# Summing the attention block's e @ x for two or three sets of rows at once in a fused attention and SwiGLU kernel on Trainium2

## The chip, the core and the metric

The kernel runs on one core of one Trainium2 chip. The core has a matrix engine (TensorE, "PE" in the profile, with its weight loads shown apart as "PEld"), a vector engine (VectorE, "DVE"), a scalar engine (ScalarE, "ACT"), a general engine (GpSimd, "POOL"), and a queue engine (SyncE, "SP") that here only issues transfers. [...]The metric is the device time of the whole kernel in microseconds, the median of several runs.

## What is computed

Two blocks follow each other. The first is an attention through 32 inducing rows, for each of 4 batches of 12416 rows of 128 numbers; the second is a gated feed-forward network over all 49664 rows.

```
def mab(q, kv):
    s = scale * (q @ kv.transpose(0, 2, 1))
    a = exp(s - s.max(-1));  a /= a.sum(-1) + 1e-9
    return a @ kv
h   = mab(inducing, x)          # per batch: 32 x 128
y   = mab(x, h)                 # per batch: 12416 x 128
xn  = y / rms(y) * rms_g
out = (silu(xn @ w_gate) * (xn @ w_val)) @ w_out     # 128 -> 1536 -> 128
```

The change is in `h`: with `e = exp(s - max)`, the unnormalised `e @ x` of a batch sums over its 12416 rows. Everything is in float32, partly by splitting numbers in parts.

## The kernel before

**Sets, units and slots.** The 97 tiles of 128 rows of a batch are cut into seven sets: five of 16 tiles, one of 15, one of 2 (`per`, lines 81 to 85). The feed-forward network walks a batch in 25 units of up to 512 rows (four to a set, one for the last rows), and each unit in 12 slots `j`, one for each 128 columns of the 1536. So a batch has 300 slots, numbered `k` from 0; four batches have 1200.

**A slot** (`slot`, lines 654 to 678) is, on TensorE: the gate product `g` (line 656), then one earlier slot's product with `w_out`, then the value product `v` (line 667), then whatever other steps the plan has put in this slot. ScalarE takes silu of `g` (line 664), VectorE multiplies it with `v` into a tile `u` (line 673). The product with `w_out` is taken some five slots later, in one of two ways. A plain one is a float32 matmul (line 605, `acc<-u,wo`; the trace shows it as two passes). A split one is three matmuls (lines 621, 623 and 605, `acc<-xn,xn`) over parts of `u` that ScalarE and GpSimd prepare (lines 643 to 649). I call these plain and split slots. When a unit's twelve products are in, VectorE adds and turns the result (lines 613 and 614) and SP stores it (line 636). SP also fetches the moving operand `a` of the next unit (line 551, four transfers, at `j` = 2 of each unit).

**The attention of the next batch runs inside the slots of the present one.** `schedule` (lines 781 to 844) is an order written out by hand: `add(k, step, ...)` puts a step behind slot `k`. For the next batch it loads `x` transposed (line 152) and makes scores; at slots 130 to 136 it takes the maximum and the exponentials; between slots 140 and 190 it forms `h`; from slot 200 on the second scores. So this happens in batches 0, 1 and 2, for batches 1, 2 and 3. The first batch's own attention stands ahead of the first slot and is not changed in what it issues.

**Forming h.** Three steps for each set `s`:
- `load_rows(b, s)` (line 135): four transfers of 32 partitions each, on SP (line 141). 256 KB each for a full set. The sets share two buffers by turns, `xn0` and `xn1`; the last set, of two tiles, has its own, `xn6`. So the load of set 2 waits until TensorE has read set 0.
- `turn_e(s)` (line 369): VectorE transposes the set's exponentials into a tile `e` of the pool `work`, which has three buffers, shared with the tiles `eT`, `z` and `aT` of the step that prepares the next units (`seam`, lines 489 to 541).
- `sum_h(s)` (line 374): for each tile of the set a matmul of 32 columns of `e` with 128 x 128 of `x` (line 384), into one of four 32-partition strips of one bank of the accumulator memory, taken by turns, so that four strips gather four partial sums. Each matmul shows as two passes. Then VectorE copies the bank to `hl` for set 0 and adds it to `hl` for the others (lines 387, 389).

Before the change the steps stand at slots 140 + 7s (turn), 143 + 7s (sum), and 97, 103, then 130 + 7s (load): seven sums at 143, 150, 157, 164, 171, 178 and 185. `fold_l`, `divide` and `turn_h`, which use the result, stand at 187, 189 and 191. The bank comes from a pool with a single buffer (`ps_m`), shared with other steps, among them `square` of the seam at slot 161.

**Which slots are split** is worked out ahead by a small budget of GpSimd's time (lines 870 to 882); the sums have no part in it, so it is the same before and after.

Of the kernel before, what the change touches and what calls it, by code (L numbers as in the profile page):

```python
# [9 lines left out]
F32 = mybir.dt.float32  # L10
# [4 lines left out]
ALU = mybir.AluOpType  # L15
# [3 lines left out]
P = 128  # L19
R = 4  # L20
# [4 lines left out]
def kernel(  # L25
# [45 lines left out]
    nc = tc.nc  # L71
    B, N, C = x.shape
    m = inducing.shape[0]
# [7 lines left out]
    full, rest = divmod(N // P, 16)  # L81
    assert N % P == 0 and full >= 2 and 0 < rest < 4
    per = [16] * (full - 1) + [15, rest + 1]
    NS = len(per)
    start = [P * sum(per[:s]) for s in range(NS)]
# [18 lines left out]
    def pool(name, bufs, **kw):  # L104
        return ctx.enter_context(tc.tile_pool(name=name, bufs=bufs, **kw))
# [8 lines left out]
    work = pool("work", 3)  # L114
    once = pool("once", 1)
# [17 lines left out]
    xnat, xT = {}, {}  # L133
# [57 lines left out]
    ps = ps_m.tile([P, 512], F32, name="mm", tag="mm")  # L191
# [10 lines left out]
    if wide:  # L202
        t = scp.tile([P, SCW], F32, name="sc")
# [89 lines left out]
    def attention(b, load_next):  # L293

        st = {}
# [7 lines left out]
        def bank():  # L303
            if flowing:
                assert not lent
                return ps_m.tile([P, 512], F32, name="mm", tag="mm")
            return ps_gv.tile([P, 512], F32, name="gv", tag="gv")
# [59 lines left out]
                nc.vector.reduce_sum(out=st["hl"][:, C:C + 1], in_=st["ls"][:, 0:k + 1], axis=AX.X)  # L367

        def turn_e(s):
            e = st["e", s] = (work.tile([P, per[s] * m], F32, name="e", tag="work") if b else  # L370
                              up.tile([P, 512], F32, name="u"))[:, 0:per[s] * m]
            nc.vector.transpose(out=e, in_=sc[b][:, cols1[s]])

        def sum_h(s):

            n = per[s]
            e, xn, hl = st.pop(("e", s)), xnat.pop((b, s)), st["hl"]
            if b or not s:
                st["ps"] = bank()
            ps = st["ps"]  # L380
            head, end = (True, True) if b else (s == 0, s + 1 == NS)
            for t in range(n):
                more = t + R < n or not b and any(per[z] > t % R for z in range(s + 1, NS))
                nc.tensor.matmul(ps[ts(t % R, m), 0:C], e[:, ts(t, m)], xn[:, t, :], start=head and t < R, stop=not more)  # L384
            rows = slice(0, min(n, R) * m)
            if end and head and s:
                nc.vector.tensor_tensor(out=hl[rows, 0:C], in0=hl[rows, 0:C], in1=ps[rows, 0:C], op=ALU.add)
            elif end and b:
                nc.vector.tensor_copy(out=hl[:, 0:C], in_=ps[:, 0:C])

        def fold_l():
# [323 lines left out]
    one = weight[1, 0]  # L715
# [27 lines left out]
    ps = f["scores"](0, f["st"]["hT"][:, 0:m], R, per2[0])  # L743
# [37 lines left out]
    def schedule(b):  # L781


        plan, marks, busy = {}, [], {}

        def add(k, step, *args):
            plan.setdefault(int(k), []).append(lambda: step(*args))
            if getattr(step, "__name__", "") == "sub_max" and args[0]:
                busy[int(k)] = 1.1

        def exponentials(k, step, first):

            groups = list(range(first, NS - 1, 2))
            for i, s in enumerate(groups):
                add(k + i, step, s, NS if s == groups[-1] else s + 2)
                if i:
                    by_tanh.add((b, k + i))
            return k

        if not b:  # L800
            add(0, weight[1, 1]["sign"])
            add(1, weight[1, 1]["lower"])
            for k, one in ((1, (2, 1)), (5, (0, 2)), (8, (1, 2)), (11, (2, 2))):
                for j, name in ((0, "power"), (1, "power_number"), (1, "upper"), (2, "upper_number"), (2, "sign"), (3, "lower")):
                    add(k + j, weight[one][name])
            for k, *one in ((2, 0, 1), (4, 1, 1), (11, 0, 2), (13, 1, 2)):
                add(k, f["stack_of"], *one)
                add(k, f["stack_low"], *one)
            for step in range(4):
                add(18 + 2 * step, split_wo, step)  # L810
            for s in range(1, NS):
                add(2 * s + 16, f["scores2"], s)
                add(2 * s + 17, f["row_max"], s)
                add(2 * s + 18, f["sub_max"], s)
            marks.append(exponentials(3 * NS + 9, f["exp2"], 1))
        if b + 1 < B:
            g = attention(b + 1, b + 2 < B)
            for k, one in enumerate(pieces[b + 1]):
                add(6 * k if b else 13 + 3.8 * k, load_channels, *one)
            add(0, g["open_"])  # L820
            for s in range(NS):
                at = 20 + 14 * s if b else 37 + 12 * s
                for k in range(R):
                    add(at + 3 * k, g["turn_x"], s, k)
                add(at + 14, g["scores1"], s)
                add(97 + 6 * s if s < 2 else 130 + 7 * s, load_rows, b + 1, s)
                add(140 + 7 * s, g["turn_e"], s)
                add(143 + 7 * s, g["sum_h"], s)
                add(200 + 7 * s, g["scores2"], s)
                add(203 + 7 * s, g["row_max"], s)  # L830
                add(204 + 7 * s, g["sub_max"], s)
            for k, name in ((126, "max1"), (128, "max2"), (130, "max3"), (187, "fold_l"), (189, "divide"), (191, "turn_h"),
                            (193, "square_h")):
                add(k, g[name])
            for i in range(2):
                add(175 + 23 * i, g["fetch"], i)
                add(197 + 7 * i, g["stack"], i)
                for k in range(R):
                    add(199 + 7 * i + k, g["place"], i, k)
            marks += [exponentials(134, g["exp1_of"], 0), exponentials(254, g["exp2"], 0)]  # L840
        if b + 2 < B:
            for k in range(215, NU * NJ, 6):
                add(k, load_channels, *pieces[b + 2].pop(0))
        return plan, marks, busy
# [3 lines left out]
    order = [(b, s) for b in range(B) for s in range(NS)]  # L848
    firsts = {s: min(u for u, one in enumerate(units) if one[0] == s) for s in range(NS)}
    for k, (b, s) in enumerate(order):  # L850
# [5 lines left out]
        for late_by, one in enumerate(following):  # L856
            for i, step in enumerate(seam(*one)):
                j = ((14, 17, 18, 21, 21, 29, 31) if k else (32, 33, 34, 35, 35, 39, 41))[i]
                n, j = divmod(j, NJ)
# [4 lines left out]
    flat = [(b, u) for b in range(B) for u in range(NU)]  # L864
    after = dict(zip(flat, flat[1:]))
    plans = [schedule(b) for b in range(B)]

    free, ready = 0.0, {}  # L870
    for b, u in flat:
        plan, marks, busy = plans[b]
        for j in range(NJ):
# [3 lines left out]
            begin = max(free, now + 2.2 * SLOT)  # L877
# [6 lines left out]
    for b in range(B):  # L884
        plan, marks, _ = plans[b]

        order = [(u, j) for u in range(NU) for j in range(NJ)]
# [72 lines left out]
```

## Time and profile before

| | |
|---|---|
| median of 4 runs | 1667.05 us (1665.98 to 1667.82) |
| the profiled execution | 1667.82 us, its span 1666.0 us |
| TensorE busy | 1652.7 us, 99% of the span |
| ScalarE, VectorE, GpSimd busy | 1236.6, 1174.8, 1158.6 us |
| granted TensorE clock | 1.000 |
| matmuls of the sums in the slots, line 384 | 582 passes |
| first slots of batches 0, 1, 2, 3 | about 57, 474, 879 and 1284 us |

How to read it: a row of a group gives line, engine, operation, output and input, shape and count, then busy time and mean duration, then the idle time of the engine ahead of these instructions and what ended it. In the timeline a row is start, length, engine, line, operation; several like instructions in a row are merged into one, with a count. Matmuls are pipelined: the length of one says little, the distance from one start to the next says what it costs. The start of a batch's slots is needed to find a slot: in batch 0 slot 143 begins at 260.95 us, slot 150 at 270.95 us, slot 178 at 312.19 us.

### The profile page before, as it was taken

Reading aid. Unit: us, or ns where it says so; the run is one execution under the profiler, and the core shown is the slowest. Engines: PE = TensorE matmul, PEld = TensorE weight load, DVE = VectorE, ACT = ScalarE, POOL = GpSimd, SP = SyncE. Lnnn points to the kernel's source line nnn. Section 1 sums busy time; section 2 is a strip of 40 time slices with the busy share of each in tenths; the row PEclk is TensorE's granted clock in tenths of the full one; section 3 lists DMA queues with packets and bytes.
Section 4 is the critical chain, followed back from the end, with each engine's and each line's share of the span. In section 5 each row is a group of like instructions: output and inputs, shape, how many; then the busy total and the mean of one; then the engine's idle time right before and its main releaser. Section 6 shows DMA issues by size and latency. Waiting matters only on the chain.

```text
span 1666.0 us, 23263 instructions
## 1 busy us (share of the span) xinstructions
PE 1652.7 (99%) x6764; PEld 1035.9 (62%) x6764; DVE 1174.8 (71%) x1961; ACT 1236.6 (74%) x2234; POOL 1158.6 (70%) x931
## 2 busy tenths in 40 slices
PE   8999999999999999999999999999999999999998
PEld 6646566655676665665566656565567666666666
DVE  4887776676767877667677777666767666666665
ACT  4557777766787777776778777867677788788786
POOL 1337766767577775776578777577657888888885
PEclk9999999999999999999999999999999999999999
DMA  6455424343354131624344313252211111111111
GB/s 255 89 77 94 83 54 107 73 95 58 64 89 65 35 83 33 134 66 88 58 70 79 57 36 82 61 124 70 51 31 35 33 35 38 32 33 39 32 38 25
DMA packets 389456, 112.40 MB, mean 67 GB/s; under 512 B 365104, under 2 KB 369744, under 8 KB 386896
## 3 DMA queue, kind: packets, MB, share of 16 engines
q1 hardware_dynamic: 388592, 110.82, 32.7%
q8 instruction: 54, 0.88, 0.2%
q14 instruction: 74, 0.61, 0.1%
q10 hardware_dynamic: 736, 0.08, 0.0%
HBM read 53.95 MB, written 27.00 MB: 49 GB/s over the span
## 4 chain that ended last, share of the span: by engine, by line
PE 97%; DVE 2%; ACT 0%; DMA 0%; issue 0%; POOL 0%; SPq 0%; DVEq 0%; POOLq 0%
PE acc L605 45%; PE gv L656 17%; PE gv L667 16%; PE u L623 5%; PE u L621 5%; PE mm L331 3%; PE mm L507 1%; PE mm L384 1%; PE gv L322 1%; DMA xn<-in_x_dram 0%; DVE u L673 0%; PE gv L331 0%; PE mm L459 0%; PE mm L473 0%; POOL rs L522 0%
## 5 line engine op out<-in xcount | busy, mean ns | idle before, releaser
L673 DVE TENSOR_TENSOR u<-silu,gv 128x512 f32<-128x512 f32 (+2 forms) x1186 | 779.9, 664 | 439.5 <-PE gv L667 226.8
L664 ACT ACTIVATE silu<-gv 128x512 f32<-128x512 f32 (+2 forms) x1186 | 691.2, 584 | 357.5 <-PE gv L656 313.9
L605 PE MATMUL acc<-u,wo 128*128 128x512 f32 (+2 forms) x1600 | 791.5, 579 | 1.2 <-DVE u L673 1.2
L667 PE MATMUL gv<-a,sv 128*128 128x512 f32 (+2 forms) x1188 | 757.8, 638 | 0.9 <-DVE u L673 0.9
L644 POOL TENSOR_TENSOR xn<-u,xn 128x512 fp32r<-128x512 f32 (+2 forms) x400 | 503.4, 1259 | 351.9 <-ACT xn L643 311.6
L649 POOL TENSOR_TENSOR xn<-hs,u 128x512 fp32r<-128x512 f32 (+2 forms) x400 | 503.4, 1258 | 40.5 <-ACT hs L648 37.0
L656 PE MATMUL gv<-a,sg 128*128 128x512 f32 (+2 forms) x1188 | 483.6, 407 | 0.0
L656 PEld LDWEIGHTS gv<-a,sg 128*128 128x128 f32 x1188 | 224.1, 189 | 227.9 <-ACT silu L664 110.1
L605 PEld LDWEIGHTS acc<-u,wo 128*128 128x128 f32 x1600 | 298.6, 188 | 78.7 <-issue 16.0
L667 PEld LDWEIGHTS gv<-a,sv 128*128 128x128 f32 x1188 | 224.0, 189 | 194.4 <-issue 133.8
L643 ACT ACTIVATE xn<-u 128x512 fp32r<-128x512 f32 (+2 forms) x400 | 247.7, 619 | 24.9 <-DVE u L673 22.8
L648 ACT ACTIVATE hs<-xn 128x512 f32<-128x512 f32 (+2 forms) x400 | 245.8, 614 | 4.7 <-POOL xn L649 3.6
L605 PE MATMUL acc<-xn,xn 128*128 128x512 f32 (+2 forms) x400 | 156.4, 391 | 0.0
L623 PE MATMUL u<-xn,xn 128*128 128x512 f32 (+2 forms) x400 | 155.6, 389 | 0.0
L621 PE MATMUL u<-xn,xn 128*128 128x512 f32 (+2 forms) x400 | 155.2, 388 | 0.0
L522 POOL TENSOR_TENSOR rs<-ms,mhalf 128x16 f32<-128x16 f32 (+2 forms) x28 | 75.9, 2710 | 16.6 <-DVE ms L520 14.7
L605 PEld LDWEIGHTS acc<-xn,xn 128*128 128x128 f32 x400 | 75.0, 187 | 19.0 <-POOL xn L649 2.4
L623 PEld LDWEIGHTS u<-xn,xn 128*128 128x128 f32 x400 | 75.1, 188 | 18.1
L621 PEld LDWEIGHTS u<-xn,xn 128*128 128x128 f32 x400 | 75.0, 188 | 16.9 <-issue 0.7
L614 DVE STREAM_TRANSPOSE o<-o 128x512 f32<-128x512 f32 (+2 forms) x97 | 67.7, 698 | 3.4
L613 DVE TENSOR_TENSOR o<-acc,o 128x512 f32<-128x512 f32 (+2 forms) x97 | 64.9, 669 | 0.0
L626 ACT ACTIVATE o<-u 128x512 f32<-128x512 f32 (+2 forms) x97 | 56.4, 582 | 0.0
(166 smaller groups left out, 775.2 us busy)
## 6 DMA issues: line engine op xcount, KB each, us to landing
out_dram<-o SPq DMA_DIRECT2D x320, 64.0 KB, 1.9
xn<-in_x_dram SPq DMA_DIRECT2D x62, 256.0 KB, 4.8
xT<-in_x_dram SPq DMA_DIRECT2D x60, 256.0 KB, 5.3
a<-hi SPq DMA_DIRECT2D x156, 64.0 KB, 2.0
a<-lo SPq DMA_DIRECT2D x156, 64.0 KB, 2.0
w<-w SPq DMA_DIRECT2D x22, 256.0 KB, 3.1
xn<-in_x_dram SPq DMA_DIRECT2D x4, 1024.0 KB, 11.7
out_dram<-o SPq DMA_DIRECT2D x64, 60.0 KB, 1.9
```

The costliest lines, as they stand in the source:

```text
L522: nc.gpsimd.tensor_tensor(out=rs, in0=ms, in1=mhalf[rows, 0:n], op=ALU.pow)
L605: nc.tensor.matmul(acc[:, 0:T], lhsT, rhs, start=st["left"] == NJ, stop=st["left"] == 1)
L621: nc.tensor.matmul(ups[:, 0:T], w[:, i, :], hi, start=st["k"] == nk, stop=False)
L623: nc.tensor.matmul(ups[:, 0:T], w[:, NK + i, :], lo, start=False, stop=not st["k"])
L643: nc.scalar.activation(hi, v, AF.Copy, scale=1.0 - 2.0 ** -13)
L644: nc.gpsimd.tensor_tensor(out=lo, in0=v, in1=hi.bitcast(F32), op=ALU.subtract)
L648: nc.scalar.activation(hs[:, 0:T], hi.bitcast(F32), AF.Copy, scale=1.0 + 2.0 ** -12)
L649: nc.gpsimd.tensor_tensor(out=d, in0=hs[:, 0:T], in1=v, op=ALU.subtract)
L656: nc.tensor.matmul(g[:, 0:T], sg[:, ts(j, P)], a[:, 0:T], start=True, stop=True)
L664: nc.scalar.activation(sl[:, 0:T], g[:, 0:T], AF.Silu)
L667: nc.tensor.matmul(v[:, 0:T], sv[:, ts(j, P)], a[:, 0:T], start=True, stop=True)
L673: nc.vector.tensor_tensor(out=t[:, 0:T], in0=sl[:, 0:T], in1=v[:, 0:T], op=ALU.mult)
```

## The change

For batches 1 to 3, `sum_h` takes several sets: 0 and 1 at slot 146, 2 and 3 at slot 160, 4, 5 and 6 at slot 174. All matmuls of a call accumulate in the same four strips; the copy or the addition to `hl` follows once. The turns move to slots 140, 143, 154, 157, 168, 171 and 172, the loads to 97, 103, 147, 148, 161, 162, and 108 for the last, small set, whose `e` takes the buffer of the tile `hT`, a single one, instead of one of `work`.

```diff
         def turn_e(s):
-            e = st["e", s] = (work.tile([P, per[s] * m], F32, name="e", tag="work") if b else
+            e = st["e", s] = (once.tile([P, P], F32, name="hT") if b and per[s] < R else
+                              work.tile([P, per[s] * m], F32, name="e", tag="work") if b else
                               up.tile([P, 512], F32, name="u"))[:, 0:per[s] * m]
             nc.vector.transpose(out=e, in_=sc[b][:, cols1[s]])

-        def sum_h(s):
-            n = per[s]
-            e, xn, hl = st.pop(("e", s)), xnat.pop((b, s)), st["hl"]
-            if b or not s:
+        def sum_h(*sets):
+            hl = st["hl"]
+            if b or not sets[0]:
                 st["ps"] = bank()
-            ps = st["ps"]
-            head, end = (True, True) if b else (s == 0, s + 1 == NS)
-            for t in range(n):
-                more = t + R < n or not b and any(per[z] > t % R for z in range(s + 1, NS))
-                nc.tensor.matmul(ps[ts(t % R, m), 0:C], e[:, ts(t, m)], xn[:, t, :], start=head and t < R, stop=not more)
-            rows = slice(0, min(n, R) * m)
-            if end and head and s:
-                nc.vector.tensor_tensor(out=hl[rows, 0:C], in0=hl[rows, 0:C], in1=ps[rows, 0:C], op=ALU.add)
-            elif end and b:
+            ps, whole = st["ps"], range(NS) if not b else sets
+            tiles = [(s, t) for s in whole for t in range(per[s])]
+            ends = [{t % R: (s, t) for s, t in order} for order in (reversed(tiles), tiles)]
+            for s in sets:
+                e, xn = st.pop(("e", s)), xnat.pop((b, s))
+                for t in range(per[s]):
+                    begin, end = (one[t % R] == (s, t) for one in ends)
+                    nc.tensor.matmul(ps[ts(t % R, m), 0:C], e[:, ts(t, m)], xn[:, t, :], start=begin, stop=end)
+            if b and sets[0]:
+                nc.vector.tensor_tensor(out=hl[:, 0:C], in0=hl[:, 0:C], in1=ps[:, 0:C], op=ALU.add)
+            elif b:
                 nc.vector.tensor_copy(out=hl[:, 0:C], in_=ps[:, 0:C])
...
-                add(97 + 6 * s if s < 2 else 130 + 7 * s, load_rows, b + 1, s)
-                add(140 + 7 * s, g["turn_e"], s)
-                add(143 + 7 * s, g["sum_h"], s)
+                add({0: 97, 1: 103, NS - 1: 108}.get(s, 133 + 7 * (s // 2 * 2) + s % 2), load_rows, b + 1, s)
+                add(172 if s == NS - 1 else 140 + 7 * (s // 2 * 2) + 3 * (s % 2), g["turn_e"], s)
...
+            for s in range(0, full, 2):
+                add(146 + 7 * s, g["sum_h"], *range(s, s + 2 if s + 2 < full else NS))
```

The program's order after the change differs from that before on TensorE, VectorE and SP alone. TensorE has the same instructions, with the matmuls of the sums in three runs for a batch instead of seven; VectorE has 12 additions to `hl` fewer; SP issues the same transfers in another order.

## Prediction

> **What bounds the kernel now.** I read the page's busy times and its chain first, then the groups of the lines that the change touches, then the timeline around three sums.
>
> ```profile
> PE 1652.7 (99%) x6764; PEld 1035.9 (62%) x6764; DVE 1174.8 (71%) x1961; ACT 1236.6 (74%) x2234; POOL 1158.6 (70%) x931
> PE 97%; DVE 2%; ACT 0%; DMA 0%; issue 0%; POOL 0%; SPq 0%; DVEq 0%; POOLq 0%
> ```
>
> TensorE is the bound, and the chain that ended last is its own order of work. A busy PE can hide gaps, so the question is what each run of matmuls costs from start to start. The groups of line 384 say that a sum waits for nothing but TensorE itself, and those of lines 387 and 389 that VectorE waits for the sum, not TensorE for VectorE:
>
> ```profile
> L384 PE MATMUL mm<-xn,e 128*32 128x128 f32 x582 | 20.7, 276 | 0.0
> L384 PEld LDWEIGHTS mm<-xn,e 128*32 128x32 f32 x582 | 15.0, 109 | 10.7 <-PE acc L605 7.3 <-DVE u L673 1.7 <-DVE z L515 1.7
> L387 DVE TENSOR_TENSOR hl<-hl,mm 128x128 f32<-128x128 f32 x15 | 4.2, 280 | 3.2 <-PE mm L384 3.2
> ```
>
> Of the 10.7 us, each of the 21 sums has about 0.5 ahead of its first weight load: something is paid at the change from 128 columns to 32. The timeline of TensorE around the sixth sum (slot 178) and the seventh (slot 185) of batch 0 prices it; the columns are start and length:
>
> ```profile
> 312.19 0.41 PE L656 MATMUL gv<-a,sg 128*128 128x512 f32 x1
> 313.14 0.40 PE L667 MATMUL gv<-a,sv 128*128 128x512 f32 x1
> 313.46 1.07 PE L384 MATMUL mm<-xn,e 128*32 128x128 f32 x30
> 314.47 0.50 PE L656 MATMUL gv<-a,sg 128*128 128x512 f32 x1
> 315.91 0.39 PE L656 MATMUL gv<-a,sg 128*128 128x512 f32 x1
> ...
> 318.56 0.39 PE L656 MATMUL gv<-a,sg 128*128 128x512 f32 x1
> 319.72 0.39 PE L656 MATMUL gv<-a,sg 128*128 128x512 f32 x1
> 321.05 0.41 PE L656 MATMUL gv<-a,sg 128*128 128x512 f32 x1
> 322.38 0.39 PE L656 MATMUL gv<-a,sg 128*128 128x512 f32 x1
> 323.64 0.41 PE L384 MATMUL mm<-xn,e 128*32 128x128 f32 x4
> 323.98 0.49 PE L656 MATMUL gv<-a,sg 128*128 128x512 f32 x1
> 325.40 0.40 PE L656 MATMUL gv<-a,sg 128*128 128x512 f32 x1
> ```
>
> A split slot without a sum takes 319.72 - 318.56 = 1.16 us, a plain one 321.05 - 319.72 = 1.33. The slot of the sum and the next one, which starts late too, take 315.91 - 312.19 = 3.72 with 30 passes: 3.72 - 1.16 - 1.33 = 1.23 us for the sum. With 4 passes they take 325.40 - 322.38 = 3.02, so 0.53. The 26 passes between them cost 0.70, or 27 ns each, and the rest, 0.53 - 4 x 0.027 = 0.42 us, is paid once for a sum, however small.
>
> **The change part by part.**
>
> *Sums joined on TensorE.* The same pairs of slots in all three batches give 1.20, 1.20, 1.21, 1.21, 1.21, 1.22 and 0.53 us for the seven sums: 7.78 for a batch. What does a second set cost inside a run? The first batch's sum, ahead of the slots, is such a run:
>
> ```profile
> 36.42 2.55 PEld L384 LDWEIGHTS gv<-xn,u 128*32 128x32 f32 x94 [0.38 <-DVE u L372]
> ```
>
> Behind its first wait, 94 weight loads of three sets run in 2.55 us, 27 ns each, with no gap at the edges of the sets: 0.87 for 32. So the two pairs cost 1.20 + 0.87 = 2.07 each, and the run of 66 passes, in a split slot, 1.22 + 0.87 + 4 x 0.027 = 2.20. Together 6.34, which is 1.44 less than 7.78. Three batches: 4.3 us. All of it is on TensorE, so on the path.
>
> *Waits at the edges of the sets.* In the first batch's run a set waits for one thing only. In the later batches the sets that arrive by late loads wait for four transfers, and an instruction that waits for many things is preceded by separate waits of the sequencer. For sets 3 and 5 these now stand inside a run. No run of this trace has that, but it has the nearest thing, the fetch of `a` that gate product 144 waits for, just behind the sum of slot 143:
>
> ```profile
> L656 PEldq EVENT_SEMAPHORE  x2: 51/51/51, 262.6 to 262.7; - x2
> L384 PEld LDWEIGHTS mm<-xn,e x32: 106/110/110, 262.4 to 263.1; 128*32 128x32 f32 x32
> ```
>
> The two waits start 0.11 us apart, so 0.22 for the pair, and they are passed at 262.63 to 262.79, some 0.4 us before the last weight load of the sum ahead of them starts: the sequencer is ahead by more than they take. I take 0; with the cover gone it is 2 pairs x 0.22 x 3 batches = 1.3 us. The Trainium skill ("TensorE: Matmul & The Clock Gate", the table at its head) gives TensorE a queue of 64. A rule that speaks against the change follows from it: in a run of 32-column pairs 64 entries are used up in an estimated 32 x 0.027 = 0.87 us, against about 2 us among the long matmuls of the slots, so a run is where the sequencer's lead is thinnest. Even so 0.87 is over 0.22. By row and rule the sum stays 4.3; without any lead it would be 3.0.
>
> *VectorE.* Twelve additions of 0.286 us go, 3.4 us; they lie under TensorE, so 0. The turns come in pairs. Turn 5 (0.67) now stands right behind a unit's closing pair (0.68 + 0.71) in slot 171. The same heap stands before the change in slot 147: the product starts at 268.75, and the next one, behind closing and turn, ends at 271.96, while TensorE goes on to slot 150 with no gap (two slots of 1.33 and 1.16, as elsewhere). New are the small turn 6 (0.24) in slot 172 and `aT` (0.70) in slot 173; behind both wait products that TensorE needs only after the 2.2 us run of slot 174. I take 0. With no cover, 0.3 us a batch, 0.9. The additions behind the runs of 160 wait until they end, and `square` (slot 161) waits for the addition, since they share the bank: 0.29 us beside the 1.1 us or more of slot 161's own products ahead of it. Covered; uncovered 0.3 x 3 = 0.9, but the two bad cases hardly come together.
>
> *The slack that the sum of slot 143 gave.* Behind the exponentials (slots 134 to 137, 2.2 us each) ScalarE is behind: 11.4 of 12 us busy from 250 to 262. The third matmul of slot 142 starts 0.06 us after GpSimd has made its operand, that of slot 144, after the sum, 1.37 after. With the sum gone it is 1.37 - 1.20 = 0.17: still no wait. I take 0, at most 0.2 x 3 = 0.6.
>
> *Loads and SP.* The loads of sets 2 and 3 are issued once the sum of slot 146 has been read, and needed in slot 160: 13 slots of 1.25 and 1.1 of the last one, 17.4 us. Before, each single load had the same 13 slots. Each takes four issues in 1.7 us and at most 5.8 us from issue to landing in this stretch, 7 in all; the channels are full then, so a second load adds an estimated 5. Two: 12 us, against 17.4. Sets 4 and 5 stand behind a unit's store (four issues, 2.6 us), 15 against 17.4, and set 5 is 6% smaller and is read 0.9 us later. Queued behind the loads on SP is the store of the unit that closes at slot 147, about 1 us later than before; its buffer is wanted again two units on. The fetches of `a` at 146 and 158 now stand ahead of the loads instead of behind them, the one at 170 comes when the loads are through. The small load at slot 108 adds four issues of 0.46 ahead of a fetch of `a`; SP is idle there for 4.4 us (208.4 to 212.75). All 0.
>
> *Sum.* The profiled execution: span 1666.0 - 4.3 = 1661.7, time 1667.82 - 4.3 = 1663.5. The median of the runs lies 0.8 below the profiled one: 1667.05 - 4.3 = 1662.75, say 1662.8 us. The smallest change that a measurement of this kernel can tell is about 0.2%, 3.3 us, so this is just beyond it. Both bounds: 26 ns a pass as within the larger sums gives 4.6 us at most; all costs taken as 0 at their upper bounds (1.3, 0.9, 0.6) leave 1.5.
>
> **The rivals.**
>
> *Part of the gain is paid back* (0.22). Waits at the edges, or late products in slots 171 to 175, or the want of slack at 144, cost 1 to 3 us in all: about 1664.8, within 0.2%. For it: three places with margins of a tenth or two of a microsecond. Against: each has a like in this trace that costs nothing.
>
> *The loads come late* (0.08), and the kernel is slower. The place is the run at slots 160 and 174, whose TensorE waits with the whole slot stream behind it. Six such waits undo 4.3 us at 0.72 us each, that is when a pair of loads takes over 18.1 us instead of 12 (with the store ahead of it, 15). At 20 us they are 2.6 us late each: 1667.05 - 4.3 + 6 x 2.6 = 1678.4. For it: nothing between the loads any more, and the second of them must wait for both sums, where before every load had its own turn. Against: 2 us and more of slack at the worst place by the trace's own durations.
>
> *The switch costs more than its two slots show* (0.04): if the drained engines behind a sum also cost something later that the pairs of slots do not hold, twelve fewer give up to 6 us, 1661.
>
> That the change does not do what it says is no case: in the program's order the runs stand joined, and the additions are gone.
>
> **How the numbers follow.** The case of the sum, 1662.0 to 1663.6, has 0.66. Faster by over 0.2% holds it and the larger gain: 0.70. The same: 0.22. Slower: 0.08. The range leaves out the late loads and the ends of the others: 1661.7 to 1665.6.
>
> **What would show it.** Right: line 384 in nine runs of 64 or 66 passes, with one idle of about 0.5 us of the weight loads each; 2.07 us for the pairs and 2.2 for the last run by the distance of the gate products; unchanged slots around them; twelve fewer rows of the addition. Wrong: a gap inside a run at pass 33 (waits at the edge), an idle TensorE put down to a transfer of `xn` (loads), or to VectorE in slots 174 to 176, or slots of 144 to 149 longer than 1.33 and 1.17.

## The result and the profile after

| | before | after |
|---|---|---|
| median | 1666.6 us (57 runs, 1665.98 to 1668.06) | 1663.53 us (37 runs, 1662.77 to 1664.95) |
| profiled execution, its span | 1667.82, 1666.0 us | 1663.5, 1661.8 us |
| first gate product to last, in that execution | 1602.64 us | 1599.11 us |

The ratio of after to before is 0.9981, with a 95% interval of 0.9977 to 0.9986. That is 3.07 us less, 0.18%: the interval lies clear of no change, but the gain is just under the 0.2% that I had called the least that can be told. The forecast was 1662.8 in a range of 1661.7 to 1665.6; the time lies in the range, 0.7 us above the forecast.

The page after, its busy times and its chain, shows the same bound:

```profile
PE 1646.6 (99%) x6764; PEld 1035.5 (62%) x6764; DVE 1173.4 (71%) x1949; ACT 1235.6 (74%) x2234; POOL 1158.2 (70%) x931
PE 96%; DVE 2%; DMA 1%; ACT 0%; issue 0%; POOL 0%; SPq 0%; DVEq 0%; POOLq 0%
```

TensorE has the same 6764 instructions and is busy 6.1 us less (3.5 of them in the slots, the rest ahead of the first slot). VectorE has the 12 additions fewer, 3.3 us, but is busy only 1.4 us less, because the 20 operations `ms<-ms` of the seam (line 522) take 12.4 us instead of 10.7. The groups of the matmul of the sums (line 384 before, 387 now) and of the addition behind them, with the shapes kept apart:

```profile
L387 PEld LDWEIGHTS mm<-xn,e 128*32 128x32 f32 x570 | 15.2, 110 | 4.5 <-issue 2.8 <-PE acc L607 1.7
L389 DVE TENSOR_TENSOR hl<-hl,mm 128x128 f32<-128x128 f32 x6 | 1.7, 288 | 3.9 <-PE mm L387 3.9
```

The idle time ahead of these weight loads fell from 10.7 us to 4.5, as 21 runs became nine: 0.51 and 0.50 us for each. Six additions are left, and they wait for the sum, not the other way round.

The timeline of TensorE in batch 0, around the run of slot 146 and that of slot 174 (start, length, engine, line, operation; line 658 is the gate product that opens a slot):

```profile
263.50 0.40 PE L658 MATMUL gv<-a,sg 128*128 128x512 f32 x1
...
264.92 1.95 PE L387 MATMUL mm<-xn,e 128*32 128x128 f32 x64
266.80 0.51 PE L658 MATMUL gv<-a,sg 128*128 128x512 f32 x1
...
304.07 0.41 PE L658 MATMUL gv<-a,sg 128*128 128x512 f32 x1
...
305.35 1.95 PE L387 MATMUL mm<-xn,e 128*32 128x128 f32 x62
307.12 0.39 PE L387 MATMUL mm<-xn,hT 128*32 128x128 f32 x4
307.44 0.50 PE L658 MATMUL gv<-a,sg 128*128 128x512 f32 x1
...
308.87 0.41 PE L658 MATMUL gv<-a,sg 128*128 128x512 f32 x1
```

Each run stands in one piece, with no gap at pass 33. Slot 146 takes 266.80 - 263.50 = 3.30 us, slot 174 takes 307.44 - 304.07 = 3.37, and slot 175 behind it 1.43, a tenth more than a plain slot, as behind every sum before. Taken as the prediction took them, by the pair of slots against the same slots without a sum, the three runs cost 2.07, 2.07 and 2.31 us a batch, 6.45 against 7.78 before. I had 2.07, 2.07 and 2.20. The three batches are alike.

Where the 3.53 us between the first gate product and the last came from: slots 140 to 200 are 1.26, 1.25 and 1.25 us shorter in the three batches (3.76 together), and slot 295 of batch 0 is 0.22 longer. That one is far from the change: it stands where the last full unit closes. VectorE's addition and turn of lines 615 and 616 come 0.2 us later there, and the value product of slot 295 and the gate product behind it wait for the multiplications (line 675) that follow them. The slot has 0.97 us instead of 0.75 in this execution and in those of all four experiments, so it goes with the changed program; which of its parts moves VectorE there against TensorE was not tried.

The span has 0.7 us more of a gain than the slots. The first gate product began at 56.85 us before and at 55.58 after, a stretch that the change does not touch and that ended between 54.99 and 55.54 in the four experiments, and the tail behind the last gate product was 0.5 us longer (7.07 against 6.54), with the same matmuls and stores at the same distances. So the span of 1661.8 against the 1661.7 that I had worked out is partly luck: in the slots I was 0.8 us out. The medians fit the slots: the profiled execution of before is itself 1.2 us above its median, about what its late first gate product makes (1.27), and without that delay the 3.53 of the slots less the 0.53 of the tail is an estimated 3.0 us, against the 3.07 of the medians. Below I compare the slots.

### The profile page after: what moved, and what is told of

Its sections match the earlier page's. It is cut to its first block, busy times and chain, and to the rows that moved or that the text cites. A ratio compares the mean times of both kernels' runs of the same rounds, so it can differ in the third digit from the quotient of the medians.

```text
span 1661.8 us, 23234 instructions
## 1 busy us (share of the span) xinstructions
PE 1646.6 (99%) x6764; PEld 1035.5 (62%) x6764; DVE 1173.4 (71%) x1949; ACT 1235.6 (74%) x2234; POOL 1158.2 (70%) x931
## 4 chain that ended last, share of the span: by engine, by line
PE 96%; DVE 2%; DMA 1%; ACT 0%; issue 0%; POOL 0%; SPq 0%; DVEq 0%; POOLq 0%
PE acc L607 45%; PE gv L658 17%; PE gv L669 16%; PE u L625 5%; PE u L623 5%; PE mm L331 3%; PE mm L509 1%; PE mm L387 1%; DMA xn<-in_x_dram 1%; DVE u L675 0%; PE mm L461 0%; PE gv L322 0%; PE mm L475 0%; POOL rs L524 0%; DMA ind<-in_inducing_dram 0%
```

## The experiments

The theory: the gain is what a change between 128-column and 32-column matmuls costs, paid once for each run (a stretch of the sum's matmuls with nothing between them) and not for each pass, with the waits at the edges of sets and the loads hidden. The rivals after the result: the gain comes from the twelve additions (VectorE); or the price belongs to something else at a run's beginning, a new bank or the instruction's turn in the queue, and not to the change of width. Beside them stood the question why the last run costs 0.11 more than I had reckoned. All four ran on one chip, beside 13 runs of the kernel before with a median of 1666.46 us. Line numbers shift by one to three between them.

**Seven runs again, all else as after.** The sets keep the shared bank, the single copy or addition, the loads and the turns; only each set's matmuls stand in a slot of their own: 145 and 146, 159 and 160, 172 to 174.

```diff
-        def sum_h(*sets):
+        def sum_h(*sets, now=None):
...
-            if b or not sets[0]:
+            if b and now in (None, sets[0]) or not b and not sets[0]:
                 st["ps"] = bank()
...
-            for s in sets:
+            for s in sets if now is None else (now,):
...
+            if now is not None and now != sets[-1]:
+                return
...
-                add(146 + 7 * s, g["sum_h"], *range(s, s + 2 if s + 2 < full else NS))
+                sets = range(s, s + 2 if s + 2 < full else NS)
+                for now in sets:
+                    add(146 + 7 * s + now - sets[-1], lambda sets=sets, now=now: g["sum_h"](*sets, now=now))
```

> The changed kernel with the matmuls of each set in a slot of its own again (145 and 146, 159 and 160, 172 to 174), but still one bank and one copy or addition for a group: seven runs, three additions. If the gain comes from fewer changes between 128 and 32 columns on TensorE, it is all given back: 4 more changes a batch at 0.33 to 0.36 us, 12 in all, +4.0 to 4.3 us over the changed kernel, within 0.1% of the kernel before. If it came from the twelve additions less on VectorE or from fewer waits for the bank, the time stays at that of the changed kernel.

Measured: 1667.42 us (10 runs, 1667.18 to 1668.94), a ratio to the kernel before of 1.0005, interval 0.9995 to 1.0015. The whole gain is gone: by the medians it is 3.89 us over the changed kernel, a little under the 4.0 to 4.3 expected. The timeline of TensorE in batch 0:

```profile
263.59 1.08 PE L387 MATMUL mm<-xn,e 128*32 128x128 f32 x32
264.60 0.50 PE L660 MATMUL gv<-a,sg 128*128 128x512 f32 x1
...
266.12 1.08 PE L387 MATMUL mm<-xn,e 128*32 128x128 f32 x32
267.13 0.51 PE L660 MATMUL gv<-a,sg 128*128 128x512 f32 x1
```

and its groups of the two lines:

```profile
L387 PEld LDWEIGHTS mm<-xn,e 128*32 128x32 f32 x570 | 14.6, 109 | 9.5 <-issue 6.7 <-DVE hT L373 1.7 <-PE acc L609 1.1
L391 DVE TENSOR_TENSOR hl<-hl,mm 128x128 f32<-128x128 f32 x6 | 1.7, 284 | 0.9 <-PE mm L387 0.9
```

The additions are six, as after, and the idle time of the weight loads is back near that of before: 9.5 us in the 18 runs of this row, 0.53 each (the small set's three runs stand in a row of their own; the part put down to the turn, line 373, is no more than the ordinary half microsecond of three runs). First gate product to last is 1603.04 us, 3.93 more than after: twelve more runs at 0.33 us each. It is 0.40 above the kernel before, of which slot 295 is 0.22. So the additions, and the loads and turns in their new places, cost or bring nothing beyond the 0.2 us that is left, and the gain is in the number of runs. It also gives the size of the fixed part without a model of passes: 0.33 us, not the 0.42 of the prediction.

**Full-width matmuls inside the runs, and narrow ones.** Does the price come with the change of width, or with a run's beginning? After each fourth tile of a run, but not at its end (20 places a batch), one more matmul of 32 columns of the identity goes into columns of the same bank that nobody reads. In one kernel it uses all 128 columns of TensorE, in the other a strip of 32 as the sum itself does.

```diff
                     nc.tensor.matmul(ps[ts(t % R, m), 0:C], e[:, ts(t, m)], xn[:, t, :], start=begin, stop=end)
+                    if b and t % R == R - 1 and (s, t) != ends[1][R - 1]:
+                        nc.tensor.matmul(ps[:, 256:288], ident[:], ident[:, 0:m], start=False, stop=False)
```

The narrow one has `ps[0:m, 256:288], ident[:, 0:m]` in place of `ps[:, 256:288], ident[:]`.

> The changed kernel with a matmul of full width (128 columns of weights, 32 columns of data, into unused columns of the same bank, read by nobody) after every fourth tile inside the runs: 20 in a batch, 60 in all. If a change of width costs, each adds 0.33 us and its own two passes (at least 0.05 us by the issue rate, up to 0.4 by the length of its two weight loads): 23 to 44 us in all. If the price belongs to the step (its waits, its addition) and not to the change of width, each adds its own passes alone, 3 to 24 us.

> The control of the run with breaks: the same 60 extra matmuls, but with 32 columns of weights, in the first strip. No change of width, so 0.05 us each by passes, or up to 0.22 if a second matmul of the same strip in a round has to wait its turn: 3 to 13 us in all, and in any case well below the full-width ones.

Measured, one run each: 1691.56 us with the full-width matmuls and 1666.57 with the narrow ones; first gate product to last 1627.62 and 1602.82 us, that is 28.5 and 3.7 more than after, each within what was expected with a price on the change of width. Over 60 places: 0.475 us and 0.06. The timeline of the full-width kernel inside the run of slot 146:

```profile
264.59 0.43 PE L387 MATMUL mm<-xn,e 128*32 128x128 f32 x8
264.94 0.41 PE L389 MATMUL mm<-ident 128*128 128x32 f32 x2
265.28 0.43 PE L387 MATMUL mm<-xn,e 128*32 128x128 f32 x8
```

From one eight of passes to the next are 265.28 - 264.59 = 0.69 us, where eight passes of an unbroken run take 0.22 (8 x 27 ns). The groups of the inserted weight loads in the two kernels, full-width first:

```profile
L389 PEld LDWEIGHTS mm<-ident 128*128 128x128 f32 x120 | 17.8, 188 | 11.9 <-issue 11.9
```

```profile
L389 PEld LDWEIGHTS mm<-ident 128*32 128x32 f32 x120 | 13.2, 110 | 0.0
```

The same count, the same bank, the identity in both: only the width differs, and the idle time ahead of the weight loads is 11.9 us with the one, 0.20 us a place, and 0.0 with the other. No wait on another engine is named. So a change of width is enough to make a price inside a run; a run's beginning and the bank are not needed. The difference between the kernels is 0.415 us a place, more than 0.33; a part of it is the longer weight load (188 ns against 110, twice a place), which these two kernels can't part from the change of width. For the size I take the 0.33 of seven runs against three. There the neighbours of a run are matmuls with 512 columns of data, unlike those put into the runs here, so that all of the 0.33 belongs to the width is likely and not shown. The Trainium skill ("TensorEngine Tiling (Array Packing)", Key Properties) says that changing the tiling mode drains TensorE; the idle 0.20 us ahead of each wide pair fits that, and a run, there and back, costs 0.33 us.

**The last set in a run of its own.** The two tiles of set 6 leave the run of slot 174 and are summed and added at slot 177.

```diff
-                add(146 + 7 * s, g["sum_h"], *range(s, s + 2 if s + 2 < full else NS))
+                add(146 + 7 * s, g["sum_h"], s, s + 1)
+            add(177, g["sum_h"], NS - 1)
...
-                nc.vector.tensor_tensor(out=hl[:, 0:C], in0=hl[:, 0:C], in1=ps[:, 0:C], op=ALU.add)
+                rows = slice(0, min(R, len(tiles)) * m)
+                nc.vector.tensor_tensor(out=hl[rows, 0:C], in0=hl[rows, 0:C], in1=ps[rows, 0:C], op=ALU.add)
```

> The changed kernel with the small set summed in a run of its own at slot 177, with its own addition: four runs a batch. By a fixed price of a run of 0.33 us and turns of four passes (0.109 each, full or not): run of slot 174 falls from 2.30 to 0.33 to 0.35 plus 16 x 0.109 = 2.07 to 2.10, the new run costs 0.53 as before the change; +0.3 a batch, +1.0 us. By the prediction's price per pass (0.42 fixed, 0.027 a pass): 2.20 - 0.11 = 2.09 and 0.53, the same 0.4 a batch against 2.20; so the two differ here only in what the run of 174 loses, 0.2 or 0.1.

Measured, one run: 1664.21 us, first gate product to last 1600.06, 0.95 more than after, 0.31 a batch. The timeline of TensorE around slots 174 and 177 of batch 0:

```profile
303.95 0.41 PE L659 MATMUL gv<-a,sg 128*128 128x512 f32 x1
...
305.22 1.95 PE L387 MATMUL mm<-xn,e 128*32 128x128 f32 x62
307.10 0.50 PE L659 MATMUL gv<-a,sg 128*128 128x512 f32 x1
...
309.69 0.39 PE L659 MATMUL gv<-a,sg 128*128 128x512 f32 x1
...
311.11 0.41 PE L387 MATMUL mm<-xn,hT 128*32 128x128 f32 x4
311.45 0.49 PE L659 MATMUL gv<-a,sg 128*128 128x512 f32 x1
312.72 0.39 PE L659 MATMUL gv<-a,sg 128*128 128x512 f32 x1
```

Slot 174 takes 307.10 - 303.95 = 3.15 us without the four passes, 0.21 less than with them. At 27 ns a pass they should be worth 0.11; at 0.109 us for a pass of a strip, and two of them one after the other, 0.22. The new run costs 1.76 - 1.32 in slot 177 and 0.09 more in slot 178, 0.53 together, and 0.53 - 0.21 = 0.32, again the price of one run.

**What the sizes follow.** A tile goes to strip `t % 4` and has two passes. In an unbroken run of full sets 32 passes cost 0.87 us, so four of them, one for each strip, cost 0.109. Let a run cost 0.109 us for each pass of its fullest strip, and a fixed price. A set of 16 tiles and one of 15 both have four tiles, eight passes, in their fullest strip: 0.87. The sums of before measured 1.20 to 1.21 and 1.22, as good as equal, though the second has two passes fewer: a fixed price of 0.33 to 0.35. The sum of two tiles has two passes in a strip, 0.22, and cost 0.53: fixed 0.31. The last run of after has 4 + 4 + 1 tiles in its first strip, 18 passes, 1.96: with 2.31 the fixed price is 0.35. All of them fit 0.33 within 0.02. By passes they do not: the fixed price would be 0.42 for the small sum and 2.31 - 66 x 0.027 = 0.53 for the last run.

That a strip's passes follow one another while the four strips run side by side fits all of this; that turns of four are served together, filled or not, would give the same sums. The timeline of the kernel with narrow matmuls speaks for the first:

```profile
264.64 0.19 PE L389 MATMUL mm<-ident 128*32 128x32 f32 x1
264.65 0.31 PE L387 MATMUL mm<-xn,e 128*32 128x128 f32 x3
264.67 0.20 PE L389 MATMUL mm<-ident 128*32 128x32 f32 x1
```

The extra matmul belongs to the first strip, and in the program the next four tiles stand behind it, strip by strip. Yet three passes of the sum start between its two passes. The records do not name the strip, but three at once fit the three other strips, which then did not wait for the first.

Loads at later slots, or the old loads with the new sums, were not tried. For them there is the trace of after alone, below.

## Why the prediction was right, and where it was off

*TensorE is the bound, and each run is paid once, whatever its size: right.* Four kernels give 0.31 to 0.35 us, and with seven runs again the time goes back.

*The price, 0.42 us fixed and 27 ns a pass: mis-sized, and this is the term of the sum that failed.* I put a line through the sums of 30 passes and of 4. Both are sums whose strips are not evenly filled. The sums of 30 and of 32 passes stood in the same trace at 1.22 and 1.20 to 1.21 us: the larger one no dearer, which contradicts 27 ns a pass. I had these numbers side by side in one line of the working and did not compare them. The pairs came out right (2.07) because I built them from full sets, where both counts agree. The run of 66 passes came out 0.11 short. The saving by these pairs of slots was 7.78 - 6.45 = 1.33 a batch instead of 1.44; the slots around them, each under 0.03 off, take another 0.07 to 0.08, so that 1.25 is left. Over three batches that is 4.3 - 3.8 = 0.5 us of the miss, slot 295 is 0.2 more: 3.5 us in the slots.

*The base.* I worked from four runs with a median of 1667.05 us; with 57 it is 1666.6. So the forecast's end was nearer to the truth than its gain: 4.3 us forecast, 3.07 measured by the medians (2.3 to 3.8 by the interval of the ratio, which takes in the 3.5 of the slots). That was luck: the 0.45 us of the base hid part of a miss of 1.2.

*The waits at the edges of the sets: right.* In after's run of slot 160 the row of the queue and that of the weight loads:

```profile
L387 PEld LDWEIGHTS mm<-xn,e x64: 106/110/110, 284.6 to 286.2; 128*32 128x32 f32 x64
L387 PEldq EVENT_SEMAPHORE  x2: 51/51/51, 284.9 to 285.0; - x2
```

The two waits for set 3 are done with at about 285.03 us, when a quarter of the 64 weight loads has started; the edge of the set lies in the middle of the run, near 285.45, and no two passes stand further apart than 0.12 us. The lead of the sequencer, which I had weighed at 0.87 us by the rule and 0.4 by the row of before (0.27 counted from the end of the second wait, 262.79, to the last weight load at 263.06), is about 0.4 here, twice what the waits take. The rule's other figure, about 2 us for 64 entries among the long matmuls, was wrong: at four or five pairs to a slot of 1.16 to 1.33 us, 32 pairs are an estimated 9 us. The sum did not rest on it, and that a run thins the lead did not matter.

*The loads: right in time, by the trace.* SP's own timeline in batch 0:

```profile
266.06 3.79 SPq L141 DMA_DIRECT2D xn<-in_x_dram  x8
270.43 3.21 SPq L638 DMA_DIRECT2D out_dram<-o  x4
...
285.56 2.62 SPq L638 DMA_DIRECT2D out_dram<-o  x4
288.28 3.81 SPq L141 DMA_DIRECT2D xn<-in_x_dram  x8
```

The eight issues for sets 2 and 3 are out by 269.85 us, the last of them starting at 269.42; no transfer of this line takes over 8.6 us to land in the slots, so all is there by 278.0: 12 us, as forecast, against the 18.5 that the run of slot 160 leaves (it starts at 284.6; I had 17.4). Sets 4 and 5, behind the store, are there by 300.3 and wanted at 305.35. In the slots TensorE never waits for `xn`. The rival of the late loads had over 6 us of room at the one place and 5 at the other.

*VectorE, the slack at 144, the turns at 171 to 173, `square` at 161: right.* Slot 144 takes 1.18 us (1.26 before, behind a sum), 147 takes 1.26 and 161 1.71, which is 0.1 more than before (1.61) and the usual tail behind a run; slots 171 and 172 are plain ones at 1.32 and 1.33.

*The rivals.* At 0.18% the time lies just on the side of "within 0.2%", to which I had given 0.22, and not on that of "faster by over 0.2%", to which I had given 0.70; still its 1664.8 was 1.3 us off and my 1662.8 was 0.7. None of the three places that this rival named pays anything back. What was paid back was a mis-sized term and slot 295, a place that no case had. The case that the switch costs more than the slots show fell: seven runs against three give less, 0.33, than I had taken.

## What to carry to other kernels

Before a line is put through two rows, look for a third row that the line must pass through: here the sums of 30 and 32 passes, which cost the same, would have shown that the count of passes does not set the time; that the count of the fullest strip does came out of the later runs. On a kernel that TensorE bounds, gather the narrow matmuls into few runs, and expect for each run saved one fixed price, 0.33 us here, and nothing for the work that other engines are spared. Take the base from more than a handful of runs when the gain is 0.2%.

## What the runs showed of the hardware

- A run of 32-column float32 matmuls between 128-column ones costs 0.33 us of TensorE's time beside its passes (twelve more runs: 3.93 us). A full-width matmul of 32 columns put into a narrow run costs 0.475 us with its own work, a narrow one 0.06; the idle 0.20 us ahead of the wide one's weight loads is put down to no wait, only to "issue".
- With four strips in use, the time of a run goes by its fullest strip, 0.109 us for a pass of 128 columns: 15 tiles cost as much as 16, and two tiles behind 31 others cost 0.21 us and not 0.11.
- The waits of TensorE's sequencer between two sets of one run, 51 ns each, were over some 0.4 us before the first pass that they guard, and cost nothing.
